# One-pass matmuls of two expert layers read and write from last to first, with one tile grown by 64 bytes

## The chip, the cores and the metric

The kernel runs on one core of a Trainium2 chip. The metric is the device time of one execution in microseconds. The kernel before takes 932.41 us, the median of 3 runs (932.18 to 933.4).

## The reference

Three layers follow each other; all inputs and the output are float32 (some weights arrive as 64-bit numbers).

```
attention, for 4 batches x 8 heads, 768 steps, 48 wide:
  scale = min(|a|, 0.999) / (|a| + 1e-6);  a = (a_re + i a_im) * scale
  for t:  S = a_t * S + k_t v_t^T  (complex);  y_t = q_t . Re(S)
x = y as 3072 tokens x 384
first MoE:   h = x @ w_in (384 x 2048);  g = h * clip(h + 3, 0, 6) / 6;  x = g @ w_out (2048 x 384)
second MoE:  a = x @ w1;  b = x @ w2 (384 x 1024);  h = (a * b) @ w3 (1024 x 1024);  out = h @ w_out2 (1024 x 384)
```

## The kernel before

All work is recorded as operations of a planner (`Plan`, with durations, due times and buffers). Its `run` decides the order of the instructions on each engine ahead of time; the chip then only runs that list. The attention recurrence is done in chunks of 128 steps with matrix products (lines 684 to 731, plain float32). Its 24 chunks are cut into seven blocks of 2, 2, 4, 4, 4, 4 and 4 chunks (256 or 512 tokens); as soon as a block is through attention, the first MoE takes it (`s1` for x @ w_in and the clip, `s2` for g @ w_out), while attention goes on with the next chunks.

Block 0 is multiplied in plain float32 (lines 867 and 898), which the records show as two passes over 256 moving rows. For all other blocks and for the second MoE each operand is split into a high part and a low part of type float32r, and a product is three matmuls of one pass each, high x high, high x low and low x high. `mm3` (lines 742 to 744) does this with the tokens as moving rows: 512 columns wide in five blocks of the first MoE (18 matmuls for each of 16 slices of the hidden layer, 1440 in all) and in the second MoE (`b1`, 6 x 8 x 18 = 864), 256 wide in block 1 (288). `fold` (lines 1041 to 1043) multiplies w3 by w_out2 ahead of time, 192 one-pass matmuls of 384 columns. `b2` (lines 1104 to 1106) multiplies by the folded weights, 576 one-pass matmuls of 384 columns; in both the weights are the moving rows. Each of these matmuls has its own weight load of 128 columns.

A moving operand or an output is a view of a tile; without a step of -1 it is read or written from the first to the last column. In the built program every weight load names its 128 columns from the last to the first (its start address is that of the last column, and its step is -1).

Tiles stand in SBUF one after another in the order in which their names first occur, each aligned to 32 bytes. What matters here is where a tile begins within 256 bytes. All slices of a tile that the matmuls use begin at multiples of 512 bytes from its start, so the tile's own place is theirs:

| tile | used as | before | with the change |
|---|---|---|---|
| `W` (also the split x of the second MoE, `xs`) | weights of the first MoE; moving rows of `b1`, `fold`, `b2` | 224 | 224 |
| `xh`, `xl`, `gh`, `gl` | moving rows of the first MoE | 160 | 224 |
| `u`, `s1`, `ai`, `ar`, `k`, `q` | weights in `b1`, `b2`; some moving rows in `fold` | 224 | 224 |
| `cs`, `Kc` | a few weights of `b1`, moving rows of `fold` | 32 | 96 |
| `Ks`, `xf` | a few weights of `b1` | 160 | 224 |

`ce` stands ahead of `cs` and all tiles below it in this order, and is 16 columns (64 bytes) wide.

Of the kernel before, what the change touches and what calls it, by code (L numbers as in the profile page):

```python
# [256 lines left out]
def c_act(n, psum=False):  # L257
    return n / 1200.0 + (0.05 if psum else 0.095)


def c_tt(n):
    return n / 960.0 + 0.07
# [10 lines left out]
def c_mm(n):  # L273
    return n / 2308.0 + 0.009
# [145 lines left out]
def main_kernel(tc, q, k, v, a_re, a_im, w_in, w_out, w1, w2, w3, w_out2, consts, qT, kT, arT, aiT, vT, wiT, woT, w1T, w2T, w3T, wo2T, out, blocks=(2, 2, 4, 4, 4, 4, 4)):  # L420
    nc = tc.nc
    act, dve, pe = nc.scalar, nc.vector, nc.tensor
# [4 lines left out]
    DM, DFF = w_in.shape  # L427
    DF2 = w1.shape[1]
    KD, KF, KI = DM // 128, DFF // 128, DF2 // 128
# [15 lines left out]
    with tc.tile_pool(name="keep", bufs=1) as kp:  # L445
      c5_ = kp.tile([128, 2, 128], F32, name="c2")
      flag = kp.tile([1, 1], I32, name="flag")
      with ctx:
# [7 lines left out]
        def WB(shape):  # L456

            return SB("W", [128, 2] + shape, NW, F32R)
# [4 lines left out]
        def PS(tag, shape, n=1, free=0):  # L463
            return P.buf("ps" + tag, lambda: ps.tile(shape, F32, tag=tag, name=tag, bufs=P.slots["ps" + tag]), n, free)
# [28 lines left out]
        def ACT(dur, fn, r, w, **kw):  # L493
            return P.add("ACT", dur, fn, r, w, **kw)

        def DVE(dur, fn, r, w, **kw):
            return P.add("DVE", dur, fn, r, w, **kw)

        def PE(dur, fn, r, w, **kw):
            return P.add("PE", dur, fn, r, w, **kw)  # L500
# [4 lines left out]
        def A(o, i, f, scale=1.0, bias=0.0, **kw):  # L505
            act.activation(out=o, in_=i, func=f, scale=scale, bias=bias, **kw)  # L506

        def TT(o, i0, i1, op):
            dve.tensor_tensor(out=o, in0=i0, in1=i1, op=op)  # L509
# [10 lines left out]
        def cut(t_, shape):  # L520

            if list(t_.shape) == list(shape):
                return t_
            names = "abc"[:len(shape) - 1]
            size = 1
            for x in shape[1:]:
                size *= x
            s_ = " ".join(names)
            return t_.rearrange("p %s -> p (%s)" % (s_, s_))[:, :size].rearrange("p (%s) -> p %s" % (s_, s_), **dict(zip(names, shape[1:])))
# [13 lines left out]
        def group(gi):  # L543
# [7 lines left out]
            def nb(name, shape=None, n=1, tag=None, full=None):  # L551
                shape = shape or [128, KD, w]
                full = full or shape[:-1] + [shape[-1] * GT // C] if name != "ys" else [128, 4, GT, 128]
                tag = tag or name
                return P.buf(tag, lambda: cut(sb.tile(full, F32, tag=tag, name=tag, bufs=P.slots[tag]), shape), BUFS.get(tag, n))
# [33 lines left out]
            ACT(cA, lambda: A(n_().bitcast(I32), th(), AF.Copy, scale=INV2PI), [th], [n_])  # L589
            DVE(cT, lambda: STT(th(), th(), INV2PI, n_().bitcast(I32), ALU.mult, ALU.subtract), [n_], [th])  # L590
            if not last:
                ce = nb("ce", [128, KD], 2, full=[128, 16])
                DVE(0.17, lambda: dve.tensor_copy(out=ce().unsqueeze(2), in_=th()[:, :, w - 1:w]), [th], [ce])
                A_prev["ce"] = ce
            cs = nb("cs", [128, 2, KD, w])
# [67 lines left out]
            bh, bl, xh, xl = xbuf[j]  # L663
            o = (u - blk[j][0]) * 128
# [74 lines left out]
                    DVE(c_tt(384), lambda: TT(o_, o_, mb(), ALU.mult), [KT], [An])  # L739

        def mm3(o, wh, wl, xh, xl, start, stop, **kw):
            pe.matmul(o, wh, xh, start=start, stop=False, **kw)  # L742
            pe.matmul(o, wh, xl, start=False, stop=False, **kw)  # L743
            pe.matmul(o, wl, xh, start=False, stop=stop, **kw)  # L744
# [95 lines left out]
        def s1(j, f):  # L840
# [22 lines left out]
            def mm():  # L863
                for kk in range(KD):
                    if whole:
                        wf = packed(w, 768)().rearrange("p (a b) -> p a b", a=shape[0])
                        pe.matmul(h()[:, :n], wf[:, kk, o:o + 128], xh()[:, kk, :n].bitcast(F32), start=kk == 0, stop=kk == KD - 1)
                    else:
                        wh, wl = part(w, 0, shape), part(w, 1, shape)
                        mm3(h()[:, :n], wh[:, kk, o:o + 128], wl[:, kk, o:o + 128], xh()[:, kk, :n], xl()[:, kk, :n], kk == 0, kk == KD - 1)  # L870
# [15 lines left out]
        def s2(j, f, g, acc, at, own):  # L886
            n = blk[j][1] * 128
            w, shape = wo[f // 2]
            gh, gl = g
            whole = j < NATIVE  # L890

            def mm():
                kw = {"skip_group_check": True} if j < FIRST else {}
                for m in range(KD):
                    a = slice(m * 128, m * 128 + 128)
                    if whole:
                        wf = packed(w, 768)().rearrange("p (a b) -> p a b", a=shape[0])
                        pe.matmul(acc[m]()[:, at:at + n], wf[:, f % 2, a], gh()[:, :n].bitcast(F32), start=f == 0 and at == 0, stop=f == KF - 1, **kw)
                    else:
                        wh, wl = part(w, 0, shape), part(w, 1, shape)  # L900
                        mm3(acc[m]()[:, at:at + n], wh[:, f % 2, a], wl[:, f % 2, a], gh()[:, :n], gl()[:, :n], f == 0 and at == 0, f == KF - 1, **kw)
            for x in acc:
                x.part = True
            PE(3 * c_m4(n) if whole else 9 * c_mm(n), mm, [w, gh, gl] + ([opened] if at else []), acc + [own] + ([] if at or f else [opened]), pin=pins["2", j, f])

        gens = [group(g) for g in range(NG)]

        def angles(parts):
# [40 lines left out]
        for js in [range(FIRST)] + [[j] for j in range(FIRST, len(blk))]:  # L949
# [3 lines left out]
            acc = [PS(f"m{m}", [128, 512]) for m in range(KD)]  # L953
# [21 lines left out]
        def half(w, p, i):  # L975

            bufs, shape = w
            if type(bufs) is list:
                t_ = bufs[i]()[:, p]
                return t_.rearrange("p (a b) -> p a b", a=KD) if shape[0] == KD else t_  # L980
            t_ = part(bufs, p, shape)
            return t_[:, :, i * 128:i * 128 + 128] if shape[0] == KD else t_[:, i]

        def of(w, i):
            return w[0][i] if type(w[0]) is list else w[0]
# [44 lines left out]
        def fold(i, th_):  # L1030
            if i % 2 == 0:
                Ws.append(WB([2, DM]))
            Wb = Ws[-1]
            pw = PS("m%d" % (i % 3), [128, 512])

            def fm():
                for c in range(8):
                    hh, ll = th_[c // 4]()[:, 0], th_[c // 4]()[:, 1]
                    a = slice((c % 4) * 128, (c % 4) * 128 + 128)
                    bh, bl = half(wo2[c // 2], 0, c % 2), half(wo2[c // 2], 1, c % 2)  # L1040
                    pe.matmul(pw()[:, :DM], hh[:, a], bh, start=(c == 0), stop=False)  # L1041
                    pe.matmul(pw()[:, :DM], hh[:, a], bl, start=False, stop=False)
                    pe.matmul(pw()[:, :DM], ll[:, a], bh, start=False, stop=(c == 7))
            PE(24 * c_mm(384), fm, th_ + [of(x, i) for x in wo2 for i in range(2)], [pw], pin=pins["f", i])
            hs = Buf(None, None)
            ACT(c_act(DM, True), lambda: A(Wb()[:, 0, i % 2], pw()[:, :DM], AF.Copy), [pw], [Wb, hs], part=True)
            DVE(c_tt(DM), lambda: TT(Wb()[:, 1, i % 2], pw()[:, :DM], Wb()[:, 0, i % 2].bitcast(F32), ALU.subtract), [pw, hs], [Wb], part=True)
# [48 lines left out]
        def b2(j, i, g, acc):  # L1096
            gh, gl = g
            Wb = Ws[i // 2]

            def mm(ts):  # L1100
                for t in ts:
                    a = slice(t * 128, t * 128 + 128)
                    o = acc[t]()[:, :DM]
                    pe.matmul(o, gh()[:, a], Wb()[:, 0, i % 2], start=(i == 0), stop=False)  # L1104
                    pe.matmul(o, gh()[:, a], Wb()[:, 1, i % 2], start=False, stop=False)  # L1105
                    pe.matmul(o, gl()[:, a], Wb()[:, 0, i % 2], start=False, stop=(i == KI - 1))  # L1106
            for t in range(len(acc)):
                PE(3 * c_mm(384), lambda t=t: mm([t]), [gh, gl, Wb], [acc[t]], pin=pins["o", j, i])

        for j, (a, n) in enumerate(two):  # L1110
# [13 lines left out]
            acc = [PS(f"m{t}", [128, 512]) if t < 3 else PS("x", [128, 512], 5) for t in range(n)]  # L1124
# [89 lines left out]
```

## Time and profile before

| | |
|---|---|
| median of 3 runs | 932.41 us |
| the profiled execution's own time | 933.94 us |
| its span, first to last instruction | 931.8 us |
| TensorE (PE) busy, share of the span | 887.6 us, 95% |
| weight loads (PEld) busy | 758.9 us, 81% |
| VectorE (DVE) busy | 586.2 us, 63% |
| ScalarE (ACT) busy | 507.7 us, 54% |

PE is TensorE's matmuls and PEld its weight loads, which run beside the matmuls. The recorded length of a matmul holds its way through the array as well, so that records of neighbours overlap; how fast the engine gets on is read from the distance between starts. The clock row gives the TensorE clock granted, in tenths of full speed.

### The profile page before, as it was taken

The numbers are of one execution on the slowest core, as the hardware profiler recorded it, in microseconds if no ns is written. First come the engines' busy times: TensorE is split into PE (matmuls) and PEld (weight loads), VectorE is DVE, ScalarE is ACT, GpSimd is POOL, SyncE is SP. The second block draws the span as 40 slices with busy tenths as digits, with TensorE's granted clock in tenths as the row PEclk, the third lists the DMA queues.
The fourth block names the chain that finished last, engine by engine and source line by source line (L and its number), as shares of the span: only waits on it lengthen the run. The fifth ranks groups of instructions, "written<-read, shape, count | busy, mean of one in ns | idle before, by whom it ended". The sixth has DMA issues, their size and how long they took to land.

```text
span 931.8 us, 13311 instructions
## 1 busy us (share of the span) xinstructions
PE 887.6 (95%) x5194; PEld 758.9 (81%) x5194; DVE 586.2 (63%) x913; ACT 507.7 (54%) x816; POOL 0.2 (0%) x4
## 2 busy tenths in 40 slices
PE   0589999999999999999999999999999999999997
PEld 0478989888878888888788888898888888888886
DVE  5999999889998677868453699653322223222221
ACT  7999888978887567656523566452222223221211
POOL 0000000000000000000000000000000000000000
PEclk9999999999999999999999999999999999999999
DMA  7785736356581645355415666230010201000001
GB/s 265 207 231 176 195 109 168 94 131 167 157 203 46 150 145 147 80 142 160 95 47 126 200 221 249 96 93 23 27 42 1 68 1 46 1 35 0 10 25 38
DMA packets 55992, 102.88 MB, mean 110 GB/s; under 512 B 6385, under 2 KB 34161, under 8 KB 55921
## 3 DMA queue, kind: packets, MB, share of 16 engines
q1 hardware_dynamic: 55920, 101.94, 37.7%
q8 instruction: 43, 0.70, 0.3%
q14 instruction: 29, 0.23, 0.1%
HBM read 64.62 MB, written 13.63 MB: 84 GB/s over the span
## 4 chain that ended last, share of the span: by engine, by line
PE 83%; ACT 7%; DVE 4%; DMA 3%; issue 1%; SPq 1%; DVEq 0%; ACTq 0%
PE x L742 13%; PE x L743 13%; PE x L744 13%; PE m L742 6%; PE m L743 6%; PE m L744 6%; PE x L693 4%; PE m L1106 3%; PE m L1104 3%; PE m L1105 3%; ACT W L506 2%; ACT u L506 2%; PE x L705 2%; PE x L710 1%; ACT L1144 1%; PE m L1041 1%
## 5 line engine op out<-in xcount | busy, mean ns | idle before, releaser
L506 ACT ACTIVATE r<-x 128x512 f32<-128x512 f32 (+1 forms) x144 | 81.9, 569 | 150.4 <-PE x L744 131.7
L509 DVE TENSOR_TENSOR r<-r,x 128x512 f32<-128x512 f32 x48 | 33.0, 688 | 178.8 <-PE x L744 178.8
L742 PE MATMUL m<-gh,W 128*128 128x512 f32 (+1 forms) x288 | 111.2, 386 | 0.6 <-ACT gh L506 0.6
L743 PE MATMUL m<-gl,W 128*128 128x512 f32 (+1 forms) x288 | 108.8, 378 | 0.9 <-DVE gl L509 0.8
L744 PE MATMUL m<-gh,W 128*128 128x512 f32 (+1 forms) x288 | 108.1, 375 | 0.0
L506 ACT ACTIVATE gh<-r 128x512 fp32r<-128x512 f32 (+1 forms) x96 | 56.6, 591 | 81.7 <-PE m L744 78.3
L742 PE MATMUL x<-xh,W 128*128 128x512 f32 x240 | 97.5, 406 | 0.0
L744 PE MATMUL x<-xh,W 128*128 128x512 f32 x240 | 94.9, 395 | 0.0
L743 PE MATMUL x<-xl,W 128*128 128x512 f32 x240 | 94.8, 395 | 0.0
L509 DVE TENSOR_TENSOR gl<-r,gh 128x512 fp32r<-128x512 f32 (+1 forms) x96 | 61.7, 642 | 45.3 <-ACT gh L506 44.0
L742 PE MATMUL x<-W 128*128 128x512 f32 (+1 forms) x228 | 84.5, 371 | 0.0
L744 PE MATMUL x<-W 128*128 128x512 f32 (+1 forms) x228 | 84.0, 369 | 0.0
L743 PE MATMUL x<-W 128*128 128x512 f32 (+1 forms) x228 | 84.0, 368 | 0.0
L880 DVE SCALAR_TENSOR_TENSOR r<-r,x 128x512 f32<-128x512 f32 (+1 forms) x96 | 60.9, 636 | 13.4 <-ACT r L506 13.0
L506 ACT ACTIVATE W<-W 128x768 f32<-128x768 f32 (+3 forms) x78 | 64.6, 850 | 4.8 <-DMA W<-in_w3T_dram 2.3
L742 PEld LDWEIGHTS m<-gh,W 128*128 128x128 f32 x288 | 54.2, 188 | 12.2 <-ACT gh L506 0.9
L743 PEld LDWEIGHTS m<-gl,W 128*128 128x128 f32 x288 | 54.2, 188 | 11.8 <-DVE gl L509 2.0
L744 PEld LDWEIGHTS m<-gh,W 128*128 128x128 f32 x288 | 54.1, 188 | 10.8
L506 ACT ACTIVATE u<-r 128x512 fp32r<-128x512 f32 x36 | 22.7, 631 | 63.7 <-DVE r L509 63.7
L742 PEld LDWEIGHTS x<-xh,W 128*128 128x128 f32 x240 | 45.1, 188 | 11.3 <-issue 0.9
L744 PEld LDWEIGHTS x<-xh,W 128*128 128x128 f32 x240 | 45.1, 188 | 10.9
L743 PEld LDWEIGHTS x<-xl,W 128*128 128x128 f32 x240 | 45.1, 188 | 9.6
(216 smaller groups left out, 1908.9 us busy)
## 6 DMA issues: line engine op xcount, KB each, us to landing
KT<-Kc SPq DMA_DIRECT2D x72, 129.0 KB, 3.5
QT<-cs SPq DMA_DIRECT2D x72, 128.0 KB, 4.3
W<-in_w3T_dram SPq DMA_DIRECT2D x16, 512.0 KB, 4.5
v<-in_vT_dram SPq DMA_DIRECT2D x24, 256.0 KB, 2.7
W<-in_wiT_dram SPq DMA_DIRECT2D x8, 768.0 KB, 7.1
W<-in_woT_dram SPq DMA_DIRECT2D x8, 768.0 KB, 6.3
ar<-in_arT_dram SPq DMA_DIRECT2D x12, 384.0 KB, 3.2
ai<-in_aiT_dram SPq DMA_DIRECT2D x12, 384.0 KB, 3.0
```

The lines of the kernel that those rows point to most:

```text
L506: act.activation(out=o, in_=i, func=f, scale=scale, bias=bias, **kw)
L509: dve.tensor_tensor(out=o, in0=i0, in1=i1, op=op)
L693: pe.matmul(p_()[:, i, :], KT()[:, 4 * g + i, tok], QT()[:, 4 * g + i, tok])
L705: pe.matmul(py()[64 * j:64 * j + 64, p, :], vb.ap[:, h, :], Pm[h // 4]()[:, h % 4, :], start=True, stop=first, tile_position=(0, 64 * j), ...
L710: pe.matmul(py()[64 * j:64 * j + 64, p, :], Ap.ap[:, h, :], QT()[:, h, tok], start=False, stop=True, tile_position=(0, 64 * j), skip_group ...
L742: pe.matmul(o, wh, xh, start=start, stop=False, **kw)
L743: pe.matmul(o, wh, xl, start=False, stop=False, **kw)
L744: pe.matmul(o, wl, xh, start=False, stop=stop, **kw)
L880: DVE(c_tt(n), lambda: dve.scalar_tensor_tensor(out=r()[:, :n], in0=r()[:, :n], scalar=6.0, in1=h()[:, :n], op0=ALU.min, op1=ALU.mult), [h ...
L1104: pe.matmul(o, gh()[:, a], Wb()[:, 0, i % 2], start=(i == 0), stop=False)
L1105: pe.matmul(o, gh()[:, a], Wb()[:, 1, i % 2], start=False, stop=False)
L1106: pe.matmul(o, gl()[:, a], Wb()[:, 0, i % 2], start=False, stop=(i == KI - 1))
```

## The change

The moving operand and the output of every one-pass matmul (`mm3`, `fold`, `b2`) are given with step -1, so that the columns are read and written from last to first. Column j of the result still lands in column j. Besides, `ce` is allocated 32 columns wide instead of 16, and all tiles behind it move up by 64 bytes (the table above). The plain float32 matmuls are left as they are.

The order of the instructions on every engine is the same as before. The waits that the framework attaches differ in places: rows on PE with a wait for PE's own count are 138 instead of 80, most of the new ones on a matmul that opens a PSUM bank anew, and some waits of VectorE have gone from one instruction to its neighbour.

```diff
             if not last:
-                ce = nb("ce", [128, KD], 2, full=[128, 16])
+                ce = nb("ce", [128, KD], 2, full=[128, 32])
...
         def mm3(o, wh, wl, xh, xl, start, stop, **kw):
+            o, xh, xl = o[:, ::-1], xh[:, ::-1], xl[:, ::-1]
             pe.matmul(o, wh, xh, start=start, stop=False, **kw)
             pe.matmul(o, wh, xl, start=False, stop=False, **kw)
             pe.matmul(o, wl, xh, start=False, stop=stop, **kw)
...
-                    pe.matmul(pw()[:, :DM], hh[:, a], bh, start=(c == 0), stop=False)
-                    pe.matmul(pw()[:, :DM], hh[:, a], bl, start=False, stop=False)
-                    pe.matmul(pw()[:, :DM], ll[:, a], bh, start=False, stop=(c == 7))
+                    o, bh, bl = pw()[:, :DM][:, ::-1], bh[:, ::-1], bl[:, ::-1]
+                    pe.matmul(o, hh[:, a], bh, start=(c == 0), stop=False)
+                    pe.matmul(o, hh[:, a], bl, start=False, stop=False)
+                    pe.matmul(o, ll[:, a], bh, start=False, stop=(c == 7))
...
-                    o = acc[t]()[:, :DM]
-                    pe.matmul(o, gh()[:, a], Wb()[:, 0, i % 2], start=(i == 0), stop=False)
-                    pe.matmul(o, gh()[:, a], Wb()[:, 1, i % 2], start=False, stop=False)
-                    pe.matmul(o, gl()[:, a], Wb()[:, 0, i % 2], start=False, stop=(i == KI - 1))
+                    o, bh, bl = acc[t]()[:, :DM][:, ::-1], Wb()[:, 0, i % 2][:, ::-1], Wb()[:, 1, i % 2][:, ::-1]
+                    pe.matmul(o, gh()[:, a], bh, start=(i == 0), stop=False)
+                    pe.matmul(o, gh()[:, a], bl, start=False, stop=False)
+                    pe.matmul(o, gl()[:, a], bh, start=False, stop=(i == KI - 1))
```

## Rows read from the trace of the kernel before

**Rows 1.** The page: busy time, and the row of the clock.

```profile
PE 887.6 (95%) x5194; PEld 758.9 (81%) x5194; DVE 586.2 (63%) x913; ACT 507.7 (54%) x816; POOL 0.2 (0%) x4
...
PEclk9999999999999999999999999999999999999999
```

**Rows 2.** Busy time by stretch; columns named in the first row.

```profile
core 0: us, PE busy (x) PEld busy (x) DVE busy (x) ACT busy (x) POOL busy (x), PEclk, DMA share, GB/s
...
100.00:150.00 50.00, 47.92 (x406) 44.12 (x406) 49.38 (x82) 42.26 (x75) 0.00 (x0) 1.00 0.61 151
...
165.00:250.00 85.00, 84.51 (x561) 70.28 (x561) 77.32 (x119) 69.10 (x110) 0.00 (x0) 1.00 0.50 133
250.00:450.00 200.00, 200.00 (x1193) 163.47 (x1191) 161.36 (x251) 134.13 (x213) 0.00 (x0) 1.00 0.52 137
...
650.00:900.00 250.00, 250.00 (x1205) 220.08 (x1204) 66.09 (x100) 59.37 (x101) 0.00 (x0) 1.00 0.07 24
```

**Rows 3.** PE's longest wait in total: us, times, longest.

```profile
PE x L684 <- DVE Kc L509: 30.8, 4, 29.3
```

**Rows 4.** Starts of matmuls in the first MoE, tail of attention done.

```profile
start us, us, engine line op out<-in xcount [idle before <-releaser]
539.65 0.40 PE L743 MATMUL x<-xl,W 128*128 128x512 f32 x1
...
544.78 0.40 PE L744 MATMUL x<-xh,W 128*128 128x512 f32 x1
```

**Rows 5.** Starts in the second MoE: weights in k, then b2, then weights in Kc.

```profile
674.67 0.39 PE L742 MATMUL x<-W,k 128*128 128x512 f32 x1
...
676.49 0.39 PE L744 MATMUL x<-W,k 128*128 128x512 f32 x1
676.71 0.33 PE L1104 MATMUL m<-W,u 128*128 128x384 f32 x1
...
678.82 0.39 PE L742 MATMUL x<-W,Kc 128*128 128x512 f32 x1
...
680.69 0.40 PE L744 MATMUL x<-W,Kc 128*128 128x512 f32 x1
```

**Rows 6.** Starts in the second MoE: weights in Ks.

```profile
685.10 0.39 PE L742 MATMUL x<-W,Ks 128*128 128x512 f32 x1
...
686.93 0.39 PE L744 MATMUL x<-W,Ks 128*128 128x512 f32 x1
```

**Rows 7.** Starts of plain float32 matmuls of block 0, six to a row.

```profile
68.02 1.46 PE L867 MATMUL x<-xh,W 128*128 128x256 f32 x6
...
71.91 0.38 PE L898 MATMUL m<-gl,W 128*128 128x256 f32 x1
```

**Rows 8.** Starts of weight loads in the first MoE, and of the matmuls beside them.

```profile
542.22 0.19 PEld L743 LDWEIGHTS m<-gl,W 128*128 128x128 f32 x1
...
542.22 0.39 PE L742 MATMUL m<-gh,W 128*128 128x512 f32 x1
542.45 0.40 PE L743 MATMUL m<-gl,W 128*128 128x512 f32 x1
```

**Rows 9.** Weight loads by shape: busy, mean ns of one, idle before.

```profile
L742 PEld LDWEIGHTS x<-xh,W 128*128 128x128 f32 x240 | 45.1, 188 | 11.3 <-issue 0.9
...
L705 PEld LDWEIGHTS x<-P,v 128*64 128x64 f32 x368 | 21.6, 136 | 7.3 <-issue 4.7 <-DVE P L509 0.5 <-DVE ai L587 0.4
```

**Rows 10.** Starts of the matmuls of fold.

```profile
605.82 0.33 PE L1042 MATMUL m<-ai,W 128*128 128x384 f32 x1
...
608.94 0.33 PE L1042 MATMUL m<-s,W 128*128 128x384 f32 x1
```

**Rows 11.** A matmul that waits for PE's own count (530.32) behind its predecessor.

```profile
530.09 0.39 PE L744 MATMUL x<-xh,W 128*128 128x512 f32 x1
530.32 0.40 PE L742 MATMUL x<-xh,W 128*128 128x512 f32 x1
```

## The prediction, made before the changed kernel ran

> **What bounds the kernel now.** I read the page first: PE is busy for 95% of the span, at the full clock in every slice, while VectorE has 63% and ScalarE 54% [rows 1]. A full clock is the 2.4 GHz level, so one column of a one-pass matmul takes 0.4167 ns, 512 columns 0.2133 us and 384 columns 0.160 us. The table by stretch shows where the bound changes: from 100 to 150 us VectorE is busy 49.4 of 50 us, from 250 on PE fills every microsecond [rows 2]. The only wait of PE worth its name is 30.8 us, of which 29.3 are one wait for the first chunk [rows 3]. So from about 165 us to the end the time is the number of matmuls times the distance between their starts, and what changes that distance changes the end one for one.
>
> That distance is longer than the columns need. In the first MoE 23 matmuls of 512 columns start within 5.13 us, 22 distances of 0.2332 us [rows 4], 20 ns over 0.2133. In the second MoE nine matmuls with weights in k start every 0.2275 us, nine with weights in Kc every 0.2338 us [rows 5], nine with weights in Ks every 0.2288 us [rows 6]; `b2` takes 2.11 us for twelve of 384 columns, 0.1758 each [rows 5], `fold` 3.12 us for 18, 0.1733 each [rows 10]. Against this stands block 0: plain float32, two passes a matmul, 256 columns at half the pace, which is again 0.2133 us of columns, and there three rows of six take 3.89 us, 0.2161 each [rows 7]. Those matmuls load 128 columns of weights each as well, so a weight load as such costs only 3 ns; what costs 11 to 18 ns more is a load beside moving rows at full pace.
>
> The load of the next weights starts together with the running matmul, both at 542.22 us [rows 8]. So both reads start in a fixed relation, and the place of their tiles within 256 bytes can matter: k and the moving rows stand both at 224 (0.2275), Kc is 192 bytes behind (0.2338), Ks 64 behind (0.2288), and the first MoE has moving rows at 160 and weights at 224, the same relation as Kc (moving minus weights 192, modulo 256), and the same 0.233. I take this as the sign that the two reads get in each other's way in places that repeat every 256 bytes.
>
> The Trainium skill, page "TensorE: Matmul & The Clock Gate", section "Step-by-step: what each phase is for", says that PE has two independent read ports and that loading the next weights takes no bandwidth from the running matmul. By that, neither place nor direction would matter, and the time would stay at 932.4; the three distances above do not agree with it.
>
> **Part 1, the place.** 64 bytes more for `ce` bring `xh`, `xl`, `gh` and `gl` from 160 to 224, the place of `W`. With both reads forward this is worth what k has over Kc, with two ends: 0.2332 down to 0.2275, or to the mean of the second MoE. That mean comes from its stretch: 1205 matmuls in 250 us [rows 2] are 0.2075 each; of 30 in a step 18 have 512 columns and 12 have 384, so (30 x 0.2075 - 12 x 0.1758) / 18 = 0.2286. Times 1440: 6.6 to 8.2 us. Kc's and Ks's few weights change place too; under 1 us, left out.
>
> **Part 2, the direction.** The trace of before holds no moving rows read backward, so its cost must be bounded. Weight loads name their columns from last to first, so moving rows now run against them. A load of 128 columns is recorded with 188 ns, one of 64 with 136 [rows 9], so a column takes 0.81 ns and the reading of 128 some 104 ns. In this time moving rows cover 104 / 0.4167 = 250 columns, 1000 bytes, and the weights 512. Against each other they pass (1000 + 512) / 256 = 5.9 times through the same place, along with each other (1000 - 512) / 256 = 1.9 times. If the excess over 0.2161 is paid by the meeting (12.5 ns / 5.9 = 2.1 ns in the second MoE, 17.1 / 5.9 = 2.9 in the first), a third of it stays. One end is that all of it goes, the other is in the rivals. I take the third, since the excess must be tied to the weights (their place moves it) and the count is the only thing that the direction surely changes.
> - First MoE, place and direction together: 0.2161 + 0.0125/3 = 0.2203 instead of 0.2332, 12.9 ns x 1440 = 18.6 us.
> - Second MoE, 512 columns: 0.2286 - 0.2203 = 8.3 ns x 864 = 7.2 us.
> - `b2`: bottom 0.160 + 0.0028 = 0.1628, excess 13.0 ns, two thirds are 8.7 ns x 576 = 5.0 us.
> - `fold`: excess 10.5 ns, 7.0 ns x 192 = 1.3 us.
> - Block 1's 288 matmuls of 256 columns: nothing, they lie where VectorE has 49.4 of 50 us [rows 2].
>
> Together 32.1 us. With no excess left it would be 24.6 + 10.8 + 7.5 + 2.0 = 44.9 us.
>
> **What takes back.** From 165 to 250 us VectorE is busy 77.3 of 85 us [rows 2]. The share of that stretch in the 18.6 us is 18.6 x 85 / 435 = 3.6 us (one-pass work of the first MoE runs from 165 to 600), PE would want 81 us, and VectorE still fits, but in a fixed order with chains; I take 1 us as lost (0 to 3.6). From 250 to 450 VectorE has 161 of 200 us, which covers PE's 8 us. The 58 added waits for PE's own count stand in front of matmuls, and behind them all of PE; but such a wait is met long before: the matmul at 530.32 has one and starts 0.23 us after its predecessor like all others [rows 11]. If each let its predecessor's whole record of 0.39 us run out instead, it would be 58 x 0.16 = 9 us; I take nothing. Transfers and other engines are as before.
>
> **The sum.** 32.1 - 1 = 31 us off the profiled execution's own 933.94 us gives 902.9. That execution is 1.5 us above the median of the runs shown, 932.41; off that it is 901.4. Forecast 901 us, its own range 886 (44.9 us, all the excess) to 916 (half of the 31).
>
> **The rivals.**
> - *Place alone counts.* The excess is paid for the share of time that both reads spend in one place, which is the same in either direction. Then only part 1 stays: 6.6 to 8.2 us, about 925. For it: place is what the trace shows, direction it doesn't. 14% (917 to 930).
> - *Nothing moves the end* (ports don't collide, or a worse new relation eats the gain): 931 to 934. Against it stand k and Kc. 8%.
> - *Held behind the weights* (slower). In the same direction the moving rows come up from behind to the place of the slower weights; if they can't pass, they go at the weights' 0.81 ns a column until the load ends. From the first meeting, half-way through, that is 52 ns in which 64 columns come instead of 125, 25 ns lost: 0.241 us for 512 columns. Cost: 7.9 ns x 1440 + 12.5 x 864 + 12.5 x 576 + 15 x 192 = 32 us, 965; held through the whole load 50 ns are lost, and the end is at about 1042. It decides from 8.1 ns a meeting on, where 1.9 meetings cost the mean of now, 0.2315. Against it: meetings cost 2 to 3 ns now. For it: both reads would start at one place, with the same step. 13%.
> - *Backward steps run at half pace* (slower), in reading rows or in writing PSUM: 512 columns take 0.427 us, and 279 + 171 + 83 + 28 = 561 us come on top, about 1493. The trace has no backward step. 5%. The Trainium skill, page "PSUM — Partial Sum Buffer", section "Specifications (TRN2)", says that PSUM has lines of 8 bytes and that any access that isn't contiguous slows matmuls significantly; a step of -1 still takes both words of a line one after the other, so I do not count it as such; no run here shows it yet.
>
> **How the numbers follow.** The forecast's case has 60%. Place alone and the forecast make 74% for faster by over 0.2% (1.9 us, about what a measurement of this kernel can tell from no change); within 0.2% 8%; slower 18%. The range for 8 in 10 runs from 886, the floor, to 934: the first three cases hold 82%, of which a few lie below the floor.
>
> **What would show it.** Starts in the first MoE every 0.220 us (forecast), 0.228 (place alone), 0.233 (nothing) or 0.24 and more (held); in the second MoE every 0.220, 0.2286 or more for 512 columns, and `b2` 0.167 instead of 0.176. Weights in Kc at 96 must then differ little from those in k, since few meetings leave little to place. Block 0 must stay at 0.216, as its matmuls are not turned. If the distances fall as said and the end does not, VectorE has taken over between 165 and 450 us, and PE will show waits for L509 and L880 there. The forecast is wrong if the distance in the second MoE, where no tile of the moving rows changes place, stays at 0.2286.

## The result and the profile after

The changed kernel takes 940.42 us, the median of 6 runs (939.82 to 941.58), against 932.63 us before (6 runs, 932.18 to 933.4): 1.0084 times the time, 95% interval 1.0071 to 1.0097. It is 0.8% slower, where 901 us were forecast.

The page of the changed kernel, busy time and clock; a profiled execution of 941.58 us, span 939.3 us. It answers to [rows 1].

```profile
PE 894.9 (95%) x5194; PEld 761.5 (81%) x5194; DVE 586.2 (62%) x913; ACT 508.8 (54%) x816; POOL 0.2 (0%) x4
...
PEclk9999999999999999999999999999999999999999
```

PE has 7.3 us more to do in the same number of matmuls, at the same clock. Where they are is shown by the starts of four matmuls of the changed kernel: the first of 512 columns, the first of `fold`, the first of the second MoE, and the last.

```profile
171.06 0.40 PE L743 MATMUL x<-xh,W 128*128 128x512 f32 x1
...
594.98 0.34 PE L1043 MATMUL m<-u,W 128*128 128x384 f32 x1
...
629.38 0.40 PE L743 MATMUL x<-W,ar 128*128 128x512 f32 x1
...
933.33 0.34 PE L1108 MATMUL x<-W,ai 128*128 128x384 f32 x1
```

In the kernel before the same four start earlier:

```profile
170.81 0.39 PE L742 MATMUL x<-xh,W 128*128 128x512 f32 x1
...
593.32 0.33 PE L1041 MATMUL m<-u,W 128*128 128x384 f32 x1
...
627.00 0.39 PE L742 MATMUL x<-W,ar 128*128 128x512 f32 x1
...
925.71 0.34 PE L1106 MATMUL x<-W,ai 128*128 128x384 f32 x1
```

So the first MoE lost 1.4 us, `fold` 0.7 us and the second MoE 5.2 us; 0.25 us lie ahead of the first of the four. The distances between starts in the changed kernel say the same. In the first MoE (25 matmuls from the first row to the second):

```profile
539.96 0.40 PE L743 MATMUL x<-xh,W 128*128 128x512 f32 x1
...
545.56 0.40 PE L743 MATMUL x<-xh,W 128*128 128x512 f32 x1
```

That is 5.60 / 24 = 0.2333 us, what it was before [rows 4], though the place has changed. In the second MoE, weights in k (nine matmuls), `b2` (twelve), weights in Kc (nine), and later weights in Ks (nine):

```profile
677.88 0.40 PE L743 MATMUL x<-W,k 128*128 128x512 f32 x1
...
679.98 0.34 PE L1106 MATMUL m<-W,u 128*128 128x384 f32 x1
...
682.11 0.40 PE L743 MATMUL x<-W,Kc 128*128 128x512 f32 x1
...
684.24 0.40 PE L743 MATMUL x<-W,q 128*128 128x512 f32 x1
...
688.47 0.40 PE L743 MATMUL x<-W,Ks 128*128 128x512 f32 x1
...
690.57 0.40 PE L743 MATMUL x<-W 128*128 128x512 f32 x1
```

k takes 2.10 / 9 = 0.2333 us instead of 0.2275, Kc 2.13 / 9 = 0.2367 instead of 0.2338 (it now stands at 96), and Ks 0.2333 instead of 0.2288; `b2` takes 2.13 / 12 = 0.1775 instead of 0.1758 [rows 5, 6]. The table by stretch shows the sum: 1185 matmuls in 250 us instead of 1205, at the same clock and with PE busy all the time; VectorE between 165 and 450 us is as busy as before [rows 2].

```profile
core 0: us, PE busy (x) PEld busy (x) DVE busy (x) ACT busy (x) POOL busy (x), PEclk, DMA share, GB/s
...
165.00:250.00 85.00, 84.62 (x564) 70.49 (x562) 77.14 (x119) 69.18 (x111) 0.00 (x0) 1.00 0.52 133
250.00:450.00 200.00, 199.91 (x1190) 163.15 (x1189) 161.29 (x250) 134.49 (x213) 0.00 (x0) 1.00 0.53 138
...
650.00:900.00 250.00, 250.00 (x1185) 217.57 (x1184) 65.41 (x99) 57.64 (x99) 0.00 (x0) 1.00 0.07 24
```

In what follows, where no two starts are shown, a distance is a mean over one-pass matmuls of 512 columns of a profiled run, taken from their starts. In the first MoE pauses of 0.245 us and more are left out. In the second MoE only matmuls whose weights stand in the rows' own place count, 702 of 864 in the kernel before. Before, the two are 0.2333 and 0.2287, with the change 0.2334 and 0.2333. "Relation" is the place of the moving rows minus the place of the weights, modulo 256 bytes.

### The profile page after: what moved, and what is told of

Same layout as the page of the kernel before. It is cut to its first block, busy times and chain, and to the rows that moved or that the text cites. A ratio compares the mean times of both kernels' runs of the same rounds, so it can differ in the third digit from the quotient of the medians.

```text
span 939.3 us, 13323 instructions
## 1 busy us (share of the span) xinstructions
PE 894.9 (95%) x5194; PEld 761.5 (81%) x5194; DVE 586.2 (62%) x913; ACT 508.8 (54%) x816; POOL 0.2 (0%) x4
## 4 chain that ended last, share of the span: by engine, by line
PE 79%; ACT 7%; DVE 6%; DMA 5%; issue 1%; SPq 1%; ACTq 0%; DVEq 0%
PE x L743 13%; PE x L744 13%; PE x L745 13%; PE m L744 5%; PE m L743 5%; PE m L745 5%; PE x L693 4%; PE m L1107 3%; PE m L1108 3%; PE m L1106 3%; ACT W L506 2%; ACT u L506 2%; PE x L705 2%; PE m L1044 1%; PE x L710 1%
## 5 line engine op out<-in xcount | busy, mean ns | idle before, releaser
L743 PE MATMUL x<-W 128*128 128x512 f32 (+1 forms) x228 | 86.0, 377 | 0.0
L744 PE MATMUL x<-W 128*128 128x512 f32 (+1 forms) x228 | 85.1, 373 | 0.0
L745 PE MATMUL x<-W 128*128 128x512 f32 (+1 forms) x228 | 85.0, 373 | 0.0
```

## The experiments

**The place alone, and the direction alone.** Each keeps one half of the change.

```diff
 e1_place:      the kernel before, with
+                ce = nb("ce", [128, KD], 2, full=[128, 32])
 e2_direction:  the changed kernel, with
+                ce = nb("ce", [128, KD], 2, full=[128, 16])
```

> The place alone: ce is 32 columns wide, all matmuls read and write forward as before. Theory P (two reads in a forward relation collide by place, the direction is a separate cost of 5 ns a matmul): the first MoE falls from 0.2332 to 0.2275 to 0.229 us between starts, the second MoE stays at 0.2286, time 6 to 8 us below before, about 925. Theory Q (the place has nothing to do with it; what differs between weights in k and in Kc is something else of these tiles): first MoE stays at 0.2332, time 932.

> The direction alone: ce is 16 columns wide as before, the one-pass matmuls read and write from last to first. Theory A (the collision goes by place in either direction, but the relation that collides least is another one when the rows run with the weights): the first MoE, moving rows at 160 and weights at 224, differs from the 0.2333 us of the changed kernel by several ns, down to 0.22 or up to 0.24; the second MoE (both at 224) stays at 0.2333. Theory B/C (a backward step has a fixed price on top of the forward place effect): the first MoE rises to 0.2332 + 0.005 = 0.238, the second stays at 0.2333, time about 947.

The place alone takes 927.53 us (4 runs) against 932.77 us, 0.9942 times, interval 0.9926 to 0.9959. The direction alone takes 939.88 us (4 runs), 1.007 times, 1.0054 to 1.0087. First and last start of a stretch of the first MoE with the place alone (89 matmuls, 0.2267 us there, 0.2278 over all):

```profile
534.91 0.39 PE L744 MATMUL x<-xh,W 128*128 128x512 f32 x1
...
554.86 0.39 PE L742 MATMUL x<-xh,W 128*128 128x512 f32 x1
```

and with the direction alone (86 matmuls, 19.83 / 85 = 0.2333 us):

```profile
535.02 0.40 PE L744 MATMUL x<-xl,W 128*128 128x512 f32 x1
...
554.85 0.40 PE L745 MATMUL m<-gh,W 128*128 128x512 f32 x1
```

So theory P holds for the place in the first MoE: 5.5 ns x 1440 = 7.9 us by these distances. Not all of it arrives: the way from the first 512-wide matmul to `fold` is 5.8 us shorter, and the medians are 5.2 us apart. Both readings of the direction fell with the second run: backward rows at 160 neither gained nor lost against those at 224. With the direction alone the relations 192, 64 and 0 all give 0.2333; read forward they give 0.2333, 0.2292 and 0.2287. Backward reading does not add to the place effect; it puts all three places at the dear end of it.

**Reading or writing.** Of the changed kernel, only one side stays backward.

```diff
 e3_read:   +            xh, xl = xh[:, ::-1], xl[:, ::-1]      (o forward; fold and b2 alike)
 e4_write:  +            o = o[:, ::-1]                         (xh, xl forward; fold and b2 alike)
```

> The changed kernel with outputs written forward and only the moving rows read backward (columns land in mirrored order, so the numbers are another computation of the same size). Theory C (reading backward costs): second MoE 0.2333 us between starts, time 940. Theory B (writing PSUM backward costs): second MoE back to 0.2286, time 925 as for the place alone.

> The changed kernel with moving rows read forward and only the outputs written backward (columns land in mirrored order, so the numbers are another computation of the same size). Theory B (writing PSUM backward costs): second MoE 0.2333 us between starts, time 940. Theory C (reading backward costs): second MoE 0.2286, first MoE 0.2275 to 0.229, time 925.

Rows read backward alone: 940.64 us (one run). Outputs written backward alone: 928.22 us (one run). The second MoE by stretch, first with backward rows and then with backward outputs:

```profile
650.00:850.00 200.00, 200.00 (x947) 173.87 (x946) 52.67 (x80) 47.36 (x81) 0.00 (x0) 1.00 0.08 26
```

```profile
650.00:850.00 200.00, 200.00 (x965) 176.06 (x964) 54.03 (x82) 48.61 (x83) 0.00 (x0) 1.00 0.08 26
```

The kernel before has 965 matmuls there, the changed one 948. Theory C holds, B falls: the price is in reading the rows, and writing PSUM from last to first costs nothing (0.2278 and 0.2289 us in the two MoEs, as for the place alone).

**Is it the meeting of two reads?** In the next pair the weights stay in one place, so that the rows pass them equally often in either direction.

```diff
 e5_still (place alone) and e6_still_back (the changed kernel):
+            wh, wl = wh[:, :1].to_broadcast([128, 128]), wl[:, :1].to_broadcast([128, 128])
 e6_still_back, block 0 as well:  xh()[:, kk, :n].bitcast(F32)[:, ::-1], gh()[:, :n].bitcast(F32)[:, ::-1]
```

> The kernel of the place alone (all reads forward, both at 224), but every weight load of a one-pass matmul reads one column 128 times (step 0), so that it stays in one place while the rows pass; another computation of the same size. Theory M (the excess over 0.2161 us is paid for meetings of two moving reads, and their number depends on their directions): 1000 bytes of rows pass a resting place 3.9 times instead of 5.9, 0.2161 + 3.9 x 0.002 = 0.224 us between starts in both MoEs. Theory R (backward reading of rows has a price of its own): no statement for forward rows but that it stays below the backward one; anything from 0.216 to 0.228.

> The changed kernel (rows and outputs backward, both at 224) with the same resting weight loads (one column read 128 times), and with the moving rows of block 0's plain float32 matmuls read backward too; another computation of the same size. Theory M: with resting weights the direction of the rows makes no difference, so the spacing is that of the forward kernel with resting weights, about 0.224 us. Theory R: backward rows cost the same whatever the weights do, 0.2333 us. Block 0, at half the pace: 0.216 us a pass pair's half as before if the price is one that half pace leaves room for, 0.233 if each backward column costs.

933.69 and 938.82 us (one run each). The rows of the two second MoEs, forward first:

```profile
650.00:850.00 200.00, 200.00 (x959) 175.32 (x958) 53.91 (x82) 48.05 (x82) 0.00 (x0) 1.00 0.08 26
```

```profile
650.00:850.00 200.00, 200.00 (x952) 173.89 (x952) 53.29 (x81) 47.78 (x82) 0.00 (x0) 1.00 0.08 26
```

Theory M falls twice. Forward rows past resting weights take 0.2313 and 0.2316 us, more than past moving ones (0.2278 and 0.2289), not the 0.224 of fewer meetings; and backward rows take 0.2333 again, with weights that rest as with weights that move. Theory R had these backward rows right, but its bound for forward ones, 0.228 us, is passed as well; why resting weights make forward rows dearer is not shown. Block 0 with backward rows keeps its distance: four rows of six, 5.18 us for 24, 0.2158 each.

```profile
66.77 1.46 PE L869 MATMUL x<-xh,W 128*128 128x256 f32 x6
...
71.95 1.46 PE L869 MATMUL x<-xh,W 128*128 128x256 f32 x6
```

So backward costs nothing at half the pace (0.2161 us in [rows 7]).

**What the excess hangs on.** Now the rows stay in one place, or go over half the bytes in the same 512 steps.

```diff
 e9_rows_still (place alone):
+            xh, xl = xh[:, :1].to_broadcast(list(o.shape)), xl[:, :1].to_broadcast(list(o.shape))
 e10_twice (place alone):
+            n2 = o.shape[1] // 2
+            xh, xl = (x[:, :n2].unsqueeze(2).to_broadcast([128, n2, 2]) for x in (xh, xl))
+            o = o.rearrange("p (a b) -> p a b", b=2)
```

> The kernel of the place alone, but the rows of mm3 are one column read 512 times (step 0), the weights as ever; fold and b2 unchanged; another computation of the same size. If the excess comes from the rows' read going from place to place beside a load: 0.216 us between starts in the first MoE. If the weight load alone makes it: 0.2278 as for the place alone.

> The kernel of the place alone, but the rows of mm3 are the first half of the columns, each read twice in a row, so that the same 512 steps go over 1024 bytes instead of 2048; fold and b2 unchanged; another computation of the same size. Rows that rest took 0.2157 us, rows that go over 2048 bytes 0.2278. If the excess is paid by the bytes that the rows' read goes over: half of it, about 0.222 us in the first MoE. If by the steps that move at all: 0.2278.

906.04 and 914.31 us (one run each). The second MoE, resting rows first:

```profile
650.00:850.00 200.00, 200.00 (x1006) 183.69 (x1005) 55.41 (x85) 49.89 (x85) 0.00 (x0) 1.00 0.08 26
```

```profile
650.00:850.00 200.00, 200.00 (x1006) 183.79 (x1005) 56.09 (x85) 49.67 (x85) 0.00 (x0) 1.00 0.08 26
```

Resting rows: 0.2157 us in the second MoE and 0.2162 in the first, all of the excess gone with the weight loads untouched. Half the bytes: 0.2157 and 0.2158 as well, neither the 0.222 of a price per byte nor the 0.2278 of a price per step. So the excess is not a toll on each byte; it is there when the rows go over 2048 bytes in 0.2133 us and gone when they go over 1024 bytes in that time, the pace of block 0. It is the pace and not the 2048 bytes: block 1's one-pass matmuls of 256 columns go over 1024 bytes at full pace, and in the kernel before those with rows in gh and gl start every 0.1158 us (121 distances), against 0.1118 with resting rows (120). Nine of them before, then nine with resting rows:

```profile
166.22 0.29 PE L742 MATMUL m<-gh,W 128*128 128x256 f32 x1
...
167.14 0.28 PE L744 MATMUL m<-gh,W 128*128 128x256 f32 x1
```

```profile
164.63 0.28 PE L743 MATMUL m<-gh,W 128*128 128x256 f32 x1
...
165.52 0.28 PE L745 MATMUL m<-gh,W 128*128 128x256 f32 x1
```

Whether moving rows would pay the excess with no weight load beside them is not shown: every matmul here has one.

Of the 8 us between the two runs, 6.9 lie in the first MoE, where PE waits longer for VectorE with half the bytes; the longest such line there, and the same line with resting rows:

```profile
PE m L746 <- DVE gl L509: 7.9, 9, 1.9
...
PE m L744 <- DVE gl L509: 3.1, 4, 1.9
```

That line makes 4.8 us of the 6.9. PE's distances are nearly the same in both, so PE's pace does not explain the difference. VectorE was slower in the run with half the bytes, in the splitting of the weights; first that run, then the one with resting rows:

```profile
L764 DVE SCALAR_TENSOR_TENSOR W<-W 128x768 int32<-128x768 int32 (+1 forms) x44 | 44.9, 1019 | 2.2 <-ACT W L506 1.4
...
L762 DVE SCALAR_TENSOR_TENSOR W<-W 128x768 int32<-128x768 int32 (+1 forms) x44 | 37.5, 853 | 1.6 <-ACT W L506 1.0
```

Why is not known, with one run of each; nor is it shown that this is what PE waits behind.

**The order of groups, and the place once more.** One run reads backward by groups of 16 bytes and forward inside them; one moves the first MoE's rows to 192; one also moves the weights of `b2`.

```diff
 e12_fours (the changed kernel):
+        def back(x):
+            return x.rearrange("p (a b) -> p a b", b=4)[:, ::-1, :]
+            o, xh, xl = back(o), back(xh), back(xl)            (fold and b2 alike)
 e7_ce24 (the kernel before):
+                ce = nb("ce", [128, KD], 2, full=[128, 24])
 e11_b2place (the kernel before):  pads of 192, 64 and 192 bytes ahead of ai, k and s1, and
+                ce = nb("ce", [128, KD], 2, full=[128, 48])
```

> The changed kernel, but the rows go backward by groups of four columns (16 bytes), forward inside a group; the output in the same order, so the result is the reference's. If what costs is going down from group to group, 0.2333 us in both MoEs as in the changed kernel; if it is the step of -1 from column to column, 0.2278 as forward.

> The kernel before with ce 24 columns wide: forward reads, moving rows of the first MoE at 192, weights at 224 (relation 224 instead of 192 before and 0 in the kernel of the place alone). If the place effect is a smooth one, the first MoE lies between 0.2333 and 0.2278, about 0.2305 us; if the same place is a special one, it stays at 0.2333.

> Place alone, and the weights of b2 moved too: pads bring ai, s1 and u to 160, so that b2's moving rows (224) stand 64 bytes ahead of its weights, the relation in which fold took 0.1717 instead of 0.1747 us; ce of 48 columns keeps the first MoE's rows at 224. All reads and writes forward. If the relation counts for 384 columns as it did in fold: b2 0.172 instead of 0.1754 us, 2 us off, some of it lost in fold, whose rows in u, s1 and ai now stand 192 behind the weights; about 926 against 927.5 for the place alone. If it was peculiar to fold: 927.5.

By groups of four: 940.8 us (one run), 947 matmuls in the stretch from 650 to 850 us, as with backward rows.

```profile
650.00:850.00 200.00, 200.00 (x947) 173.90 (x946) 52.66 (x80) 47.42 (x81) 0.00 (x0) 1.00 0.08 26
```

It is the way from group to group that counts, not the step inside one. Rows at 192: 933.62 us (one run) and 0.2331 us in the first MoE, so 32 bytes beside the weights' place nearly all of the gain is gone; there is no slope towards it. But the weights' place is not the only cheap one, nor always cheap. Forward, 512 columns take 0.2292 us at the relation 64, and 0.2324 to 0.2338 at 32, 128, 160, 192 and 224. With the place alone, weights in Ks and xf went from the relation 64 to 0 and became dearer, from 0.2292 to 0.2305 and 0.2312 us. Block 1's 256 columns with rows in gh and gl became dearer too, from 0.1158 at the relation 192 to 0.1195 at 0 (122 distances); nine of them with the place alone, to be held against the nine of the kernel before above:

```profile
165.51 0.28 PE L742 MATMUL m<-gh,W 128*128 128x256 f32 x1
...
166.47 0.28 PE L744 MATMUL m<-gh,W 128*128 128x256 f32 x1
```

The kernel with `b2` moved: 927.17 us (5 runs), 0.9942 times the kernel before, interval 0.9928 to 0.9955. `b2` fell from 0.1756 us (the mean between its neighbours, before and with the place alone) to 0.1733, some two thirds of what was hoped for, and 1.3 us by the sum; against the place alone, in other runs, that can't be told from nothing. Its row of the second MoE has 968 matmuls instead of 965:

```profile
650.00:850.00 200.00, 200.00 (x968) 176.06 (x967) 54.03 (x82) 48.64 (x83) 0.00 (x0) 1.00 0.08 26
```

The best kernels are these two, 0.6% faster than before and 1.4% faster than the changed one, and both read forward.

## Why the prediction was wrong

- **What bounds.** Right: the end moved by what the distances moved. 864 x 4.6 ns in the second MoE, 576 x 2.3 in `b2` and 192 x 3.8 in `fold` are 4.0 + 1.3 + 0.7 = 6.0 us of the 7.6 between the last starts. 1.4 us came in the first MoE, whose distance is 0.2334 instead of 0.2333; a wait of 0.9 us for a transfer (KT) that PE did not have before is among them, the rest is not settled.

```profile
PE x L693 <- DMA KT<-Kc: 0.9, 1, 0.9
```

- **Part 1, the place.** Right in size for the distances of the first MoE with forward rows: 6.6 to 8.2 us foreseen, 7.9 by the distances, of which 5.2 us are seen between the medians. The reading behind it, that two reads in one place are cheap, was too simple. It took weights in k as the case of the same place. In the changed kernel the new place was worth nothing, because backward rows have no cheap place among 0, 64 and 192. I had priced the two halves as independent, and they are not. That the same place alone does not make a matmul cheap could be read in the trace of before: nine matmuls with weights in ar, which stands at 224 like k, start every 1.85 / 8 = 0.2313 us.

```profile
672.59 0.39 PE L742 MATMUL x<-W,ar 128*128 128x512 f32 x1
...
674.44 0.39 PE L744 MATMUL x<-W,ar 128*128 128x512 f32 x1
```

- **Part 2, the direction.** This is the step that failed: "If the excess over 0.2161 is paid by the meeting", a third stays. The count of meetings was worked out from durations, but nothing in the trace tied the excess to it; that the place moved part of it was taken for all of it. With resting weights forward rows lost 2.7 to 3.5 ns instead of gaining, with resting rows the excess vanished. What the runs show in its place: the excess belongs to rows that go from place to place at full pace, up to 17.6 ns for 512 columns; the relation to the weights takes 4 to 6 ns off it at 0 and 64, and only when the rows are read forward. So 18.6 + 7.2 + 5.0 + 1.3 us forecast became 0 in the first MoE and a loss of 6.0 us behind it.
- **What takes back.** The waits added for PE's own count are free as supposed: the 47 matmuls behind the first 512-wide one, in the first MoE, that have one only in the changed kernel start 0.2120 us after their predecessors instead of 0.2116. The 1 us for VectorE was not tested by the change, since PE did not get faster. The two runs in which it did, to 0.2157 us, have waits of 3.1 and 7.9 us for VectorE's gl, so that 1 us was probably too little; at the forecast's 0.2203 it was not measured.
- **The range.** Its ends are too low by its own terms: 932.4 less 44.9 is 887.5, not 886, and 901.4 with half of 31 on top is 917, not 916. The 940.42 us measured lie above these, and above the 934 for 8 in 10 runs.
- **The rivals.** "Place alone counts" had the place right and the direction wrong. "Nothing moves the end" named a relation that eats the gain, and in the first MoE that is what is seen. "Held behind the weights" had the sign but not the mechanism, for backward rows take 0.2333 us past resting weights too. "Backward steps run at half pace" had the right seat, reading, and a price of 0.2 us where it is 0.005; its other half, writing PSUM backward, is free. That agrees with the reading given there of the Trainium skill, page "PSUM — Partial Sum Buffer", section "Specifications (TRN2)": a step of -1 does not count as an access that isn't contiguous. The number for it is that of outputs written backward, 0.2278 and 0.2289 us, as forward.
- **What would show it.** The last test named the right place, the second MoE, where the moving rows do not move. As worded it asked only whether the distance stays at 0.2286; it did not stay but rose to 0.2333, against the forecast all the same.

What stays open is why forward rows at the relations 0 and 64 are cheaper for 512 columns, what else moves the distance within one relation, and why going down takes the gain away; the runs tell which reads matter, not what happens between them.

## What to carry to other kernels

Read the distance between matmul starts against the columns' own time before changing anything, and find what the excess hangs on by resting one operand at a time (step 0); two such runs would have told here that resting the rows takes the excess away and resting the weights does not. An effect of place that is measured in one direction says nothing of the other, so two halves of a change that act on the same read are to be priced together. Where rows of four bytes are read in one pass, it paid here to read 512 and 384 columns forward, and to give the first MoE's 512 columns the weights' place within 256 bytes. For 256 columns that place was the dearer one (0.1195 against 0.1158 us), and for the 384 of `b2` the relation 64 was the better one (0.1733 against 0.1756), so the place has to be measured for each width.

## What the runs showed of the hardware that was not expected

- One-pass float32r rows over 2048 bytes take longer than their 0.2133 us of columns: 0.2267 to 0.2338 us for 512 columns by the tiles that rows and weights stand in, 0.2333 when read backward in the relations 0, 64 and 192, and 0.2157 with rows that rest or go over 1024 bytes.
- The cheap relation depends on the width: forward, 0 is cheaper than 192 for 512 columns (0.2278 against 0.2333 us) and dearer for 256 (0.1195 against 0.1158).
- Backward rows 128 bytes from the weights are dearer still, 0.2361 us against 0.2324 forward; with resting weights they take 0.2334.
- Writing PSUM from last to first is free (0.2278 and 0.2289 us), and so is reading backward in two-pass float32 (0.2158).
